# Narrower expert token blocks, weight rests by an adding DMA, and a shifted decode schedule in an attention, MoE and SoLU kernel

## The chip, the core and the metric

The kernel runs as one program on one core of a Trainium2 chip. Its time is the device time of that core in microseconds (us); lower is better. Engines are named as in the profile: PE is the matrix engine (PEld its weight loads), DVE the vector engine, ACT the scalar engine, POOL the GpSimd engine, SP the engine that here only issues DMAs.

## What is computed

Three stages in a row on 1536 tokens of width 384: a linear attention with decay, a mixture of eight experts of which each token goes to one, and a SoLU block. In short:

```python
# attention: per head a 48x48 state, y_t = r_t @ (state + u*k_t v_t), state = w*state + k_t v_t
logits = x @ w_gate                      # 1536 x 8
e = argmax(logits); gate = softmax(logits)[e]
disp[e, 0:count_e] = x[tokens of e]      # at most capacity = 384 tokens for one expert
h = relu(disp @ w1)                      # per expert 384 -> 1024
y = h @ w2                               # per expert 1024 -> 384
x2 = gate * y, back in the tokens' order
h2 = x2 @ w_in; s = h2 * softmax(h2)     # w_in, w_out are stored as float64
out = (layernorm(s) * g_ln) @ w_out
```

With the inputs used, the eight experts get 193, 174, 187, 195, 184, 203, 209 and 191 tokens.

## The kernel before

**Number form.** Float32 values are split into a rounded part `hi` (type F32R, a float32 type that PE takes in one pass) and a rest `lo`, also F32R. A product is three matmuls: hi times hi, hi times lo, lo times hi. So weights, tokens and the hidden layer all need a `hi` (made by ACT) and a `lo` (raw minus hi, made by DVE or POOL).

**Experts.** Every expert works on W = 256 columns, that is, slots for 256 tokens; tokens above W would be done by `overflow()`, which runs only if an expert has more than W. The work is cut into 32 groups g (eight experts, four groups of 256 hidden units each). The loop has steps g = 0 to 33. In step g stand:

- `mm1(g)`: 18 matmuls of 256 columns into `hps`; ACT makes `hh` from it (relu), DVE `hl`.
- `mm2(g - 2)`: 18 matmuls of 256 columns from `hh`, `hl` into `yps`. At the last group of an expert ACT and DVE write `yThi` and `yTlo`, at a column that is read from a register.
- `split_q(1, g + 4)` and `split_q(2, g + 2)`: ACT makes `whi` (L109), DVE or POOL `wlo` (L111) of one 128x768 piece of w1 and of w2. Of the w2 pieces every other one has its `wlo` from POOL, 16 in the program with one of w1; the other 48 are DVE's.
- `xe_split(e + 1)` once an expert (at step 2 for expert 1, then at every second step of an expert): PE transposes the next expert's gathered tokens (`xt`), ACT and DVE make `xhi` and `xlo`. `load_xe` gathers the tokens with an indirect DMA from POOL; its row numbers `ids` come from DRAM, where the last attention block's scatter puts them.
- `load_half`: a 768 KB half of an expert's w1 or w2 into one of four `raw` buffers, from SP.
- `load_piece`, `decode_early`, `decode_piece`: the float64 words of w_in and w_out, 16 pieces of 384 KB, are loaded (two buffers), turned by two ACT operations and four DVE operations into float32 (`da`), and split into `w_hi` and `w_lo`. Piece p is loaded at step 2p - 1, behind the weights of that step on SP (the first two from ACT), its ACT operations come at step 2p + 1, its DVE operations at step 2p + 2. The first step that decodes is step 2, the last 32.
- small work: memsets of `yT` and the scatters `inv` from POOL, position sums from DVE.

Order on each engine is the order of the code, written out by hand; every engine takes its instructions in that order, so an instruction that waits holds up all behind it on its engine. PSUM has four buffers shared by `hps` and `xt`, and two for `yps`.

**Before and after the experts.** Attention takes 12 blocks of 128 tokens; in it six weight pieces of the first expert are split already. The SoLU block takes 12 tiles: `h2` (18 matmuls of 512 columns), softmax and norm, eight transposes `st`, and `out2` (24 matmuls of 384 columns).

Of the kernel before, what the change touches and what calls it, by code (L numbers as in the profile page):

```python
# [24 lines left out]
KF = DF // 128  # L25
W = 256
WARM = 14
# [6 lines left out]
def rwkv_moe_solu_kernel(  # L34
# [20 lines left out]
    NX = NE * RS  # L55
    YW = N + W

# [18 lines left out]
    tot = const.tile([128, NE], F32, name="tot")  # L76
    NB = RS // 128
    ids = const.tile([128, NE, NB], I32, name="ids")

    def load_ids(a, b, c=0, d=2):  # L80
        s = idx.rearrange("(e b p) o -> p e (b o)", p=128, b=NB)
        for i in range(c, d):
            nc.sync.dma_start(out=ids[:, a:b, i], in_=s[:, a:b, i])

    def load_xe(e, r0, nb, rows=N + 1):
        t = xe_p.tile([128, nb, DM], F32, tag="xe", name=f"xe{e}_{r0}", bufs=1)
        for b in range(nb):
            c = r0 // 128 + b
            nc.gpsimd.indirect_dma_start(  # L89
                out=t[:, b, :], out_offset=None, in_=xs[0:rows, :],  # L90
                in_offset=bass.IndirectOffsetOnAxis(ap=ids[:, e, c:c + 1], axis=0), bounds_check=rows - 1, oob_is_err=False,
            )
        return t
# [10 lines left out]

    def split_q(kind, g, pool_lo, defer=False):
        raw = raw_t[kind, g // 2][:, (g % 2) * 768:(g % 2 + 1) * 768]
        hi = wsp.tile([128, 768], F32R, tag=f"hi{kind}", name=f"whi{kind}_{g}")
        lo = wsp.tile([128, 768], F32R, tag=f"lo{kind}", name=f"wlo{kind}_{g}")
        S.activation(hi, raw, AF.Copy)  # L109
        def low():  # L110
            (G if pool_lo else V).tensor_tensor(lo, raw, hi.bitcast(F32), ALU.subtract)  # L111

        if not defer:
            low()
        n = 3 if kind == 1 else 2
        (w1s if kind == 1 else w2s)[g] = tuple(t.rearrange("p (a f) -> p a f", a=n) for t in (hi, lo))
        return low


    def attention(actx):  # L120
# [470 lines left out]
        m = NM - 1  # L591
        x0 = ps_s.tile([128, KD, W], F32, tag="s", name="x0")

# [13 lines left out]
        for kk in range(KD):  # L607
            for bb in range(2):
                T.matmul(
                    x0[:, kk, bb * 128:(bb + 1) * 128], xe0[:, bb, kk * 128:(kk + 1) * 128], ident,  # L610
                    is_transpose=True, start=kk % 2 == 0 and bb == 0, stop=False, skip_group_check=True,
                )
# [30 lines left out]
    def experts_and_solu():  # L643
# [85 lines left out]
        def xe_split(e, t):  # L729
            hi = xe_p.tile([128, KD, W], F32R, tag="xhi", name=f"xhi{e}")  # L730
            lo = xe_p.tile([128, KD, W], F32R, tag="xlo", name=f"xlo{e}")
            for bb in range(2):
                ps = ps_t.tile([128, KD, 128], F32, tag="t", name=f"xt{e}_{bb}")
                for kk in range(KD):
                    T.transpose(ps[:, kk], t[:, bb, kk * 128:(kk + 1) * 128], ident)
                sl = slice(bb * 128, (bb + 1) * 128)
# [64 lines left out]
        def load_piece(p, eng=nc.sync):  # L801
            t = dec_p.tile([128, 384, 2], I32, tag="w64", name=f"w64_{p}")
            s = (w_in if p < NP else w_out).rearrange("p a f -> p (a f)").bitcast(I32)
            j = p % NP
            eng.dma_start(out=t.rearrange("p n c -> p (n c)"), in_=s[:, j * 768:(j + 1) * 768])
            pieces[p] = t
# [10 lines left out]
        def decode_piece(p):  # L817
            raw = pieces.pop(p)
            low, high = raw[:, :, 0], raw[:, :, 1]
            a = dec_p.tile([128, 384], I32, tag="da", name=f"da{p}")  # L820
# [35 lines left out]
        xraw = load_xe(1, 0, 2)  # L856
        dec = None
        for g in range(NQ + 2):
            e, q = divmod(g, 4)
            if q == 0 and e + 1 < YW // W:  # L860
                for n in range(2):
                    for x in range(2):
                        G.memset(yT[x][n][:, :, (e + 1) * W:(e + 2) * W].bitcast(F32), 0.0)
            if g < NQ:
# [3 lines left out]
                if g < 2:  # L868
                    split_q(2, g + 2, not g)
            if g >= 2:  # L870
                mm2(g - 2)
                if g + 2 < NQ:
                    split_q(2, g + 2, g % 2 == 0)
            if q == (1 if e else 2) and e + 1 < NE:
                xe_split(e + 1, xraw)
                if e + 2 < NE:
                    xraw = load_xe(e + 2, 0, 2)
            if g % 2 and g < NQ:
                j = (g + 1) // 2
# [11 lines left out]
            if g == 9 + NM:  # L891
                G.dma_start(out=inv_sb, in_=inv.rearrange("(m p) o -> p (m o)", p=128))
            if g in (1, 2):
                load_piece(g - 1, S)
            if g == 2:
                load_half(1, 4, S)
            if dec:
                decode()
            if g == 2 or g % 2 and 3 <= g <= 4 * NP:
                decode_early((g - 1) // 2)  # L900
            if g % 2 == 0 and 2 <= g < 2 + 4 * NP:
                dec = decode_piece(g // 2 - 1)
                decode()
            if g % 2 and 3 <= g and g // 2 + 1 < 2 * NP:
                load_piece(g // 2 + 1)

# [123 lines left out]
        def overflow():  # L1030
            load_ids(0, NE, 2, NB)
            for e in range(NE):
# [99 lines left out]
```

## Time and profile before

| | |
|---|---|
| median of 3 runs | 374.98 us (372.25 to 375.23) |
| the profiled execution's own time | 369.29 us |
| its span, first to last instruction | 367.5 us, mean granted clock 0.985 |
| PE, PEld busy | 338.4, 303.9 us |
| DVE, ACT, POOL busy | 261.8, 188.6, 173.1 us |
| bytes moved | 53.49 MB, mean 146 GB/s |

Busy time is the time in which an engine has at least one instruction under way. Matmuls overlap, so a busy PE is best judged by the distance between the starts of its matmuls. `ns` is the mean duration of one instruction, `xN` how many of them a row stands for. In a timeline a row begins with its start in us from the span's start and its length in us; in square brackets stands how long the engine was idle ahead of it, and what it waited for. Most reading is done in the stretch from 91 to 245.5 us, where the experts run.

### The profile page before, as it was taken

To read this page: it belongs to the slowest core of one execution; us is meant where nothing else is said; L and a number is where in the kernel's file an instruction comes from. 1 tells how busy PE (TensorE), PEld (TensorE's weight loads), DVE (VectorE), ACT (ScalarE), POOL (GpSimd) and SP (SyncE) were. 2 spreads that over 40 slices of the span, in tenths; PEclk is the share of its full clock that TensorE was granted. 3 is DMA by queue.
4 is the path that set the end of the run, shared out by engine and by line. 5 is a ranking of instruction groups with operands and counts; after the bars stand their busy time and mean duration, and the time that the engine had idled before them with its cause. 6 is when DMAs were issued, how large, how long until landed. Compare 5 with 4: busy or idle time off the path is not lost.

```text
span 367.5 us, 7165 instructions
## 1 busy us (share of the span) xinstructions
PE 338.4 (92%) x2637; PEld 303.9 (83%) x2637; DVE 261.8 (71%) x567; ACT 188.6 (51%) x400; POOL 173.1 (47%) x202
## 2 busy tenths in 40 slices
PE   6889999998969999999998979999999999999970
PEld 2567776766869999999998979998899999999970
DVE  8888898975648999899889989965755444444400
ACT  1355546664636777557566486532465444444410
POOL 7957778854392725567767222201343333333420
PEclk9999999999989999999999999999999999999995
DMA  6957999834367655896988755100000000000010
GB/s 227 353 176 229 254 366 310 211 108 164 49 249 265 229 210 135 185 284 173 259 218 232 244 201 172 47 0 1 2 16 29 21 21 23 22 23 21 22 51 22
DMA packets 17996, 53.49 MB, mean 146 GB/s; under 512 B 5729, under 2 KB 7394, under 8 KB 17954
## 3 DMA queue, kind: packets, MB, share of 16 engines
q1 hardware_dynamic: 14914, 45.86, 41.4%
q0 software_dynamic: 2608, 5.53, 4.6%
q10 hardware_dynamic: 432, 1.57, 1.2%
q8 instruction: 23, 0.38, 0.5%
q14 instruction: 19, 0.16, 0.2%
HBM read 48.21 MB, written 4.74 MB: 144 GB/s over the span
## 4 chain that ended last, share of the span: by engine, by line
PE 46%; DVE 27%; DMA 10%; issue 8%; POOL 2%; ACT 2%; SPq 1%; POOLq 0%; DVEq 0%; ACTq 0%
PE h L929 14%; PE hps L756 7%; DVE wlo L111 6%; PE o L997 3%; PE o L998 3%; PE o L999 3%; DMA w<-in_w_in 3%; PE yps L743 3%; PE yps L744 3%; PE yps L742 3%; PE st L988 2%; DVE w_lo L841 2%; DVE hl L763 2%; DMA u_sb<-in_u 2%; DVE A L286 2%
## 5 line engine op out<-in xcount | busy, mean ns | idle before, releaser
L111 POOL TENSOR_TENSOR wlo<-raw,whi 128x768 fp32r<-128x768 f32 x16 | 30.1, 1885 | 53.3 <-ACT whi L109 51.0
L743 PE MATMUL yps<-hl,whi 128*128 128x256 f32 x192 | 54.5, 284 | 0.1
L742 PE MATMUL yps<-hh,whi 128*128 128x256 f32 x192 | 54.4, 283 | 0.0
L744 PE MATMUL yps<-hh,wlo 128*128 128x256 f32 x192 | 54.4, 283 | 0.0
L109 ACT ACTIVATE whi<-raw 128x768 fp32r<-128x768 f32 x64 | 52.1, 840 | 3.8 <-PE yps L743 3.3
L963 POOL TENSOR_SCALAR e<-e,nmu 128x1024 f32<-128x1024 f32 x12 | 13.5, 1125 | 75.7 <-DVE nmu L962 75.7
L111 DVE TENSOR_TENSOR wlo<-raw,whi 128x768 fp32r<-128x768 f32 x48 | 46.5, 981 | 0.9 <-ACT whi L109 0.6
L940 DVE TENSOR_REDUCE nm<-h 128x1 f32<-128x1024 f32 (+1 forms) x13 | 14.8, 1141 | 33.2 <-PE h L929 33.2
L743 PEld LDWEIGHTS yps<-hl,whi 128*128 128x128 f32 x192 | 36.9, 192 | 0.3 <-DVE hl L763 0.3
L744 PEld LDWEIGHTS yps<-hh,wlo 128*128 128x128 f32 x192 | 36.9, 192 | 0.0
L742 PEld LDWEIGHTS yps<-hh,whi 128*128 128x128 f32 x192 | 36.9, 192 | 0.0
L756 PE MATMUL hps<-xhi,whi 128*128 128x256 f32 x192 | 30.2, 294 | 4.4 <-DVE hl L763 4.0
L997 PE MATMUL o<-w_hi,shi 128*128 128x384 f32 x96 | 33.1, 345 | 0.0
L998 PE MATMUL o<-w_lo,shi 128*128 128x384 f32 x96 | 32.2, 335 | 0.0
L999 PE MATMUL o<-w_hi,slo 128*128 128x384 f32 x96 | 32.2, 335 | 0.0
L756 PEld LDWEIGHTS hps<-xhi,whi 128*128 128x128 f32 x192 | 25.9, 196 | 5.7 <-DVE hl L763 5.0
L763 DVE SCALAR_TENSOR_TENSOR hl<-hps,hh 128x512 fp32r<-128x512 f32 x32 | 22.3, 698 | 10.1 <-ACT hh L762 8.4
L89 POOL DMA_INDIRECT xe<-xs,ids x16 | 20.9, 1305 | 17.5 <-DMA ids<-idx 9.3
L756 PE MATMUL hps<-xhi,wlo 128*128 128x256 f32 x192 | 28.3, 284 | 0.0
L756 PE MATMUL hps<-xlo,whi 128*128 128x256 f32 x192 | 28.3, 283 | 0.0
L756 PEld LDWEIGHTS hps<-xhi,wlo 128*128 128x128 f32 x192 | 25.5, 193 | 0.0
L756 PEld LDWEIGHTS hps<-xlo,whi 128*128 128x128 f32 x192 | 25.3, 192 | 0.0
(182 smaller groups left out, 835.4 us busy)
## 6 DMA issues: line engine op xcount, KB each, us to landing
raw<-in_w SPq DMA_DIRECT2D x31, 768.0 KB
kvr<-in_kvr SPq DMA_DIRECT2D x12, 576.0 KB
rkT<-in_rkT SPq DMA_DIRECT2D x12, 512.0 KB
w<-in_w_out SPq DMA_DIRECT2D x8, 384.0 KB
xs<-xg SPq DMA_DIRECT2D x12, 192.0 KB
w<-in_w_in SPq DMA_DIRECT2D x6, 384.0 KB
w<-in_w_in ACTq DMA_DIRECT2D x2, 384.0 KB
raw<-in_w ACTq DMA_DIRECT2D x1, 768.0 KB
```

Source lines behind the costliest of these rows:

```text
L89: nc.gpsimd.indirect_dma_start(out=t[:, b, :], out_offset=None, in_=xs[0:rows, :], in_offset=bass.IndirectOffsetOnAxis(ap=ids[:, e, c:c + ...
L109: S.activation(hi, raw, AF.Copy)
L111: (G if pool_lo else V).tensor_tensor(lo, raw, hi.bitcast(F32), ALU.subtract)
L742: T.matmul(ps, w[0][ws], x[0][xsl], start=first, stop=False, skip_group_check=True)
L743: T.matmul(ps, w[0][ws], x[1][xsl], start=False, stop=False, skip_group_check=True)
L744: T.matmul(ps, w[1][ws], x[0][xsl], start=False, stop=last, skip_group_check=True)
L756: T.matmul(ps[:, f], w1s[g][i][:, kk, wf], x[j][:, kk], start=not (i or j or f or kk), stop=j == 1 and kk == KD - 1, skip_group_check=True,)
L763: V.scalar_tensor_tensor(hl, ps, 0.0, hh.bitcast(F32), ALU.max, ALU.subtract)
L929: T.matmul(ps[j], col(x, kk, ts_), wi[w][:, kk, fs], start=not (i or kk), stop=i == 2 and kk == KD - 1,)
L997: T.matmul(ps, hi[:, f % 4], wo[0][:, f], start=f == 0, stop=False)
L998: T.matmul(ps, hi[:, f % 4], wo[1][:, f], start=False, stop=False)
L999: T.matmul(ps, lo[:, f % 4], wo[0][:, f], start=False, stop=f == KF - 1)
```

## The change

`W` becomes 224 and a token block is cut into 128 and 96 rows (`BW`). All `hps`, `yps`, `hh`, `hl`, `xhi`, `xlo` and `yT` blocks follow: 224 columns where 256 stood. No expert has more than 209 tokens, so `overflow()`, which would now have two blocks instead of one, doesn't run in either kernel.

`split_q` has a new way for the rest, `by_dma`: ACT makes `hi` and then a second piece, `lo` = minus the raw value rounded in the same way, and a DMA from POOL's queue adds the raw weights from DRAM onto `lo`. Eight pieces are made so: one in attention, and w2 pieces 6, 10, ... 30 (issued at g = 4, 8, ... 28). All others are DVE's: 56 against 48, and POOL makes none.

Float64 pieces have three buffers; pieces 0 and 1 are loaded from SP ahead of the loop, piece p at step 2p - 3 ahead of that step's weights; their ACT operations come at step 2p - 1 and DVE's at step 2p, two steps sooner. Expert 1's `xe_split` moves from step 2 to step 3, and in step 4 `mm2(2)` stands ahead of `mm1(4)`.

```diff
-W = 256
+W = 224
+BW = (128, W - 128)
...
-    def split_q(kind, g, pool_lo, defer=False):
+    def split_q(kind, g, by_dma, defer=False):
...
         S.activation(hi, raw, AF.Copy)
         def low():
-            (G if pool_lo else V).tensor_tensor(lo, raw, hi.bitcast(F32), ALU.subtract)
+            if by_dma:
+                s = (w1 if kind == 1 else w2)[g // 4, :, g // 2 % 2, (g % 2) * 768:(g % 2 + 1) * 768]
+                G.dma_start(out=lo, in_=s, accum_op=ALU.add)
+            else:
+                V.tensor_tensor(lo, raw, hi.bitcast(F32), ALU.subtract)
+        if by_dma:
+            S.activation(lo, raw, AF.Copy, scale=-1.0)
...
-            for bb in range(2):
-                ps = ps_t.tile([128, KD, 128], F32, tag="t", name=f"xt{e}_{bb}")
+            for bb, n in enumerate(BW):
+                ps = ps_t.tile([128, KD, n], F32, tag="t", name=f"xt{e}_{bb}")
                 for kk in range(KD):
-                    T.transpose(ps[:, kk], t[:, bb, kk * 128:(kk + 1) * 128], ident)
+                    T.transpose(ps[:, kk], t[0:n, bb, kk * 128:(kk + 1) * 128], ident[0:n, 0:n])
...
-            t = dec_p.tile([128, 384, 2], I32, tag="w64", name=f"w64_{p}")
+            t = dec_p.tile([128, 384, 2], I32, tag="w64", name=f"w64_{p}", bufs=3)
...
+        load_piece(0)
+        load_piece(1)
         for g in range(NQ + 2):
...
+            if g == 4:
+                mm2(g - 2)
             if g < NQ:
                 mm1(g)
                 if g + 4 < NQ:
                     split_q(1, g + 4, False)
                 if g < 2:
-                    split_q(2, g + 2, not g)
+                    split_q(2, g + 2, False)
             if g >= 2:
-                mm2(g - 2)
+                if g != 4:
+                    mm2(g - 2)
                 if g + 2 < NQ:
-                    split_q(2, g + 2, g % 2 == 0)
-            if q == (1 if e else 2) and e + 1 < NE:
+                    split_q(2, g + 2, g % 4 == 0)
+            if q == (1 if e else 3) and e + 1 < NE:
                 xe_split(e + 1, xraw)
...
+            if g % 2 and g // 2 + 2 < 2 * NP:
+                load_piece(g // 2 + 2)
...
-            if g in (1, 2):
-                load_piece(g - 1, S)
...
-            if g == 2 or g % 2 and 3 <= g <= 4 * NP:
-                decode_early((g - 1) // 2)
-            if g % 2 == 0 and 2 <= g < 2 + 4 * NP:
-                dec = decode_piece(g // 2 - 1)
+            if g % 2 == 0 and g < 4 * NP:
+                if not g:
+                    decode_early(0)
+                dec = decode_piece(g // 2)
                 decode()
-            if g % 2 and 3 <= g and g // 2 + 1 < 2 * NP:
-                load_piece(g // 2 + 1)
+            if g % 2 and g // 2 + 1 < 2 * NP:
+                decode_early(g // 2 + 1)
```

What this does to the order of instructions, at three places. First PE, around expert 1's transposes `xt`; `hps` rows are `mm1`, `yps` rows are `mm2`. Before, where step 2 ends and step 3 begins:

```order
L744 MATMUL yps_1_1627<-hh_1550,wlo_0_930 128x256
L735 MATMUL xt_0_1652<-ident,xe_0_1520 128x128 x3
L735 MATMUL xt_1_1658<-ident,xe_0_1520 128x128 x3
L756 MATMUL hps_1687<-xhi_1466,whi_3_1238 128x256 x6
L756 MATMUL hps_1687<-xhi_1466,wlo_3_1239 128x256 x6
L756 MATMUL hps_1687<-xlo_1467,whi_3_1238 128x256 x6
L742 MATMUL yps_2_1626<-hh_1583,whi_1_1035 128x256
```

Of the change, where step 3 ends and step 4 begins (of step 4's 18 `yps` matmuls the first three stand here):

```order
L754 MATMUL yps_1_1649<-hl_1601,whi_1_1035 128x224
L755 MATMUL yps_1_1649<-hh_1600,wlo_1_1036 128x224
L746 MATMUL xt_0_1736<-ident,xe_0_1521 128x128 x3
L746 MATMUL xt_1_1742<-ident,xe_0_1521 128x96 x3
L753 MATMUL yps_2_1648<-hh_1640,whi_2_1563 128x224
L754 MATMUL yps_2_1648<-hl_1641,whi_2_1563 128x224
L755 MATMUL yps_2_1648<-hh_1640,wlo_2_1564 128x224
```

The transposes stand one step (36 matmuls) later, behind group 1's `mm2`, and group 2's `mm2` follows them, not a `mm1`.

Second POOL, from expert 1's token gather on; before:

```order
L89 DMA xe_0_1520<-xs,ids 128x384 x2
L863 MEMSET yThi_1503 128x2x256
L863 MEMSET yTlo_1505 128x2x256
L863 MEMSET yThi_1504 128x256
L863 MEMSET yTlo_1506 128x256
L111 TENSOR_TENSOR wlo_2_1559<-raw_1_927,whi_2_1558 128x768
L111 TENSOR_TENSOR wlo_4_1647<-raw_2_1341,whi_4_1646 128x768
L89 DMA xe_0_1664<-xs,ids 128x384 x2
```

Of the change, from the second gather (expert 2's) on:

```order
L92 DMA xe_0_1748<-xs,ids 128x384
L92 DMA xe_0_1748<-xs,ids 96x384
L876 MEMSET yThi_1504 128x2x224
L876 MEMSET yTlo_1506 128x2x224
L876 MEMSET yThi_1505 128x224
L876 MEMSET yTlo_1507 128x224
L118 DMA wlo_6_1816<-in_w 128x768
L92 DMA xe_0_1902<-xs,ids 128x384
```

Where POOL had a subtraction of 128x768 in every second step it now has a DMA issue of that size in every fourth.

Third SP, from the row numbers `ids` of experts 1 and later on (`w` are float64 pieces, `raw` expert weights); before:

```order
L83 DMA ids<-idx 128x1x1 x2
L83 DMA ids<-idx 128x6x1 x2
L102 DMA raw_3_1595<-in_w 128x1536
L102 DMA raw_5_1736<-in_w 128x1536
L102 DMA raw_4_1738<-in_w 128x1536
L805 DMA w_2_1745<-in_w_in 128x768
```

Of the change:

```order
L85 DMA ids<-idx 128x1x1
L85 DMA ids<-idx 96x1x1
L816 DMA w_0_1528<-in_w_in 128x768
L816 DMA w_1_1530<-in_w_in 128x768
L85 DMA ids<-idx 128x6x1
L85 DMA ids<-idx 96x6x1
L816 DMA w_2_1612<-in_w_in 128x768
L105 DMA raw_3_1614<-in_w 128x1536
L816 DMA w_3_1755<-in_w_in 128x768
```

Two float64 pieces stand ahead of the row numbers of experts 2 to 7, and from then on each piece stands ahead of its step's weights.

## Rows read from the trace of the kernel before

**Rows 1.** Windows: stretch, its length, busy us PE, PEld, DVE, ACT, POOL, clock, DMA.

```profile
91.00:105.00 14.00, 9.89 (x76) 9.50 (x77) 7.01 (x13) 6.64 (x11) 6.95 (x8) 0.95 0.45 129
105.00:178.00 73.00, 73.00 (x604) 72.89 (x602) 67.56 (x116) 49.08 (x87) 41.34 (x41) 0.99 0.72 215
178.00:245.50 67.50, 63.42 (x517) 62.03 (x516) 60.19 (x87) 40.24 (x71) 23.55 (x19) 1.00 0.59 173
245.50:367.50 122.00, 110.54 (x601) 100.51 (x600) 52.76 (x105) 47.69 (x90) 35.44 (x49) 0.97 0.06 21
```

**Rows 2.** Timeline of PE: matmuls of 256 columns.

```profile
152.88 0.28 PE L742 MATMUL yps<-hh,whi 128*128 128x256 f32 x1
...
153.48 0.28 PE L744 MATMUL yps<-hh,wlo 128*128 128x256 f32 x1
```

**Rows 3.** Groups by shape: one of the six kinds of expert matmul.

```profile
L742 PE MATMUL yps<-hh,whi 128*128 128x256 f32 x192 | 54.4, 283 | 0.0
```

**Rows 4.** Timeline of PE: matmuls of 384 and of 512 columns.

```profile
301.92 0.34 PE L997 MATMUL o<-w_hi,shi 128*128 128x384 f32 x1
...
303.48 0.33 PE L997 MATMUL o<-w_hi,shi 128*128 128x384 f32 x1
...
247.08 0.85 PE L929 MATMUL h<-w_hi,yTlo 128*128 128x512 f32 x3
...
249.13 0.61 PE L929 MATMUL h<-w_hi,yTlo 128*128 128x512 f32 x2
```

**Rows 5.** Transposes of 128 columns: timeline of PE, and their group by shape.

```profile
299.98 1.03 PE L988 MATMUL st<-ident,e 128*128 128x128 f32 x8
...
L988 PE MATMUL st<-ident,e 128*128 128x128 f32 x96 | 12.4, 272 | 0.0
```

**Rows 6.** Chain around expert 1's tokens, and a window behind it (columns of rows 1).

```profile
97.74 6.49 DMA xe<-xs,ids
...
104.28 1.54 PE xt L735 x6
105.82 2.73 PE hps L756 x18
...
104.30:105.50 1.20, 1.20 (x7) 1.19 (x7) 0.00 (x0) 0.28 (x1) 1.20 (x1) 0.50 0.00 0
```

**Rows 7.** Timeline of PE: another expert's transposes.

```profile
155.04 0.82 PE L735 MATMUL xt<-ident,xe 128*128 128x128 f32 x6
```

**Rows 8.** Waits of PE's weight loads, 91 to 245.5 us: total, times, longest.

```profile
PEld hps L756 <- DVE hl L763: 5.0, 5, 1.4
PEld xt L735 <- DMA xe<-xs,ids: 4.3, 1, 4.3
```

**Rows 9.** Timelines of POOL and DVE: the same subtraction beside POOL's, and alone.

```profile
154.78 1.89 POOL L111 TENSOR_TENSOR wlo<-raw,whi 128x768 fp32r<-128x768 f32 x1 [4.02 <-ACT whi L109]
...
154.88 2.21 DVE L841 TENSOR_TENSOR w_lo<-da,w_hi 128x384 fp32r<-128x384 f32 x1
...
115.14 0.55 DVE L841 TENSOR_TENSOR w_lo<-da,w_hi 128x384 fp32r<-128x384 f32 x1
```

**Rows 10.** Groups by shape on DVE, 91 to 245 us.

```profile
L841 DVE TENSOR_TENSOR w_lo<-da,w_hi 128x384 fp32r<-128x384 f32 x8 | 11.1, 1391 | 0.0
L837 DVE SCALAR_TENSOR_TENSOR w_lo<-da,g_sb,w_hi 128x384 fp32r<-128x384 f32 x7 | 10.7, 1535 | 0.1
L785 DVE TENSOR_TENSOR yTlo<-yps,yThi 128x512 f32 x6 | 4.1, 685 | 0.0
L785 DVE TENSOR_TENSOR yTlo<-yps,yThi 128x256 f32 x6 | 2.5, 416 | 0.0
```

**Rows 11.** Chain: two `wlo` of DVE in a row, and the slowest float64 load.

```profile
150.18 1.74 DVE wlo L111 x2
...
152.36 10.10 DMA w<-in_w_in
```

**Rows 12.** Timeline of ACT: two `whi` in a row.

```profile
96.51 1.57 ACT L109 ACTIVATE whi<-raw 128x768 fp32r<-128x768 f32 x2
```

More of the change, by code (lines that the diff above doesn't have):

```diff
@@ L55, in rwkv_moe_solu_kernel @@
     NX = NE * RS
-    YW = N + W
+    YW = N + max(W, 128 * NOV)
     const = ctx.enter_context(tc.tile_pool(name="const", bufs=1))
@@ L76, in rwkv_moe_solu_kernel, with load_xe @@
     tot = const.tile([128, NE], F32, name="tot")
-    NB = RS // 128
+    NB = 2 + NOV
     ids = const.tile([128, NE, NB], I32, name="ids")
     def load_ids(a, b, c=0, d=2):
-        s = idx.rearrange("(e b p) o -> p e (b o)", p=128, b=NB)
+        s = idx.rearrange("(e r) o -> r (e o)", r=RS)
         for i in range(c, d):
-            nc.sync.dma_start(out=ids[:, a:b, i], in_=s[:, a:b, i])
-    def load_xe(e, r0, nb, rows=N + 1):
-        t = xe_p.tile([128, nb, DM], F32, tag="xe", name=f"xe{e}_{r0}", bufs=1)
+            r0, n = (i * 128, BW[i]) if i < 2 else (W + (i - 2) * 128, 128)
+            nc.sync.dma_start(out=ids[0:n, a:b, i], in_=s[r0:r0 + n, a:b])
+    def load_xe(e, c0, nb, rows=N + 1):
+        t = xe_p.tile([128, nb, DM], F32, tag="xe", name=f"xe{e}_{c0}", bufs=1)
         for b in range(nb):
-            c = r0 // 128 + b
+            c = c0 + b
+            n = BW[c] if c < 2 else 128
             nc.gpsimd.indirect_dma_start(
-                out=t[:, b, :], out_offset=None, in_=xs[0:rows, :],
-                in_offset=bass.IndirectOffsetOnAxis(ap=ids[:, e, c:c + 1], axis=0), bounds_check=rows - 1, oob_is_err=False,
+                out=t[0:n, b, :], out_offset=None, in_=xs[0:rows, :],
+                in_offset=bass.IndirectOffsetOnAxis(ap=ids[0:n, e, c:c + 1], axis=0), bounds_check=rows - 1, oob_is_err=False,
             )
@@ L591, in attention @@
         m = NM - 1
-        x0 = ps_s.tile([128, KD, W], F32, tag="s", name="x0")
+        x0 = ps_s.tile([128, KD, 256], F32, tag="s", name="x0")[:, :, 0:W]
         wps = ps_y.tile([128, 512], F32, tag="y", name="wps1")
@@ L607, in attention @@
         for kk in range(KD):
-            for bb in range(2):
+            for bb, n in enumerate(BW):
                 T.matmul(
-                    x0[:, kk, bb * 128:(bb + 1) * 128], xe0[:, bb, kk * 128:(kk + 1) * 128], ident,
+                    x0[:, kk, bb * 128:bb * 128 + n], xe0[0:n, bb, kk * 128:(kk + 1) * 128], ident[0:n, 0:n],
                     is_transpose=True, start=kk % 2 == 0 and bb == 0, stop=False, skip_group_check=True,
@@ L731, in xe_split @@
             lo = xe_p.tile([128, KD, W], F32R, tag="xlo", name=f"xlo{e}")
-            for bb in range(2):
-                ps = ps_t.tile([128, KD, 128], F32, tag="t", name=f"xt{e}_{bb}")
+            for bb, n in enumerate(BW):
+                ps = ps_t.tile([128, KD, n], F32, tag="t", name=f"xt{e}_{bb}")
                 for kk in range(KD):
-                    T.transpose(ps[:, kk], t[:, bb, kk * 128:(kk + 1) * 128], ident)
-                sl = slice(bb * 128, (bb + 1) * 128)
+                    T.transpose(ps[:, kk], t[0:n, bb, kk * 128:(kk + 1) * 128], ident[0:n, 0:n])
+                sl = slice(bb * 128, bb * 128 + n)
                 S.activation(hi[:, :, sl], ps, AF.Copy)
@@ L819, in decode_piece @@
             low, high = raw[:, :, 0], raw[:, :, 1]
-            a = dec_p.tile([128, 384], I32, tag="da", name=f"da{p}")
+            a = dec_p.tile([128, 384], I32, tag="da", name=f"da{p}", bufs=1)
             af = a.bitcast(F32)
@@ L857, in experts_and_solu @@
         dec = None
+        load_piece(0)
+        load_piece(1)
         for g in range(NQ + 2):
             e, q = divmod(g, 4)
-            if q == 0 and e + 1 < YW // W:
+            if q == 0 and (e + 1) * W < YW:
                 for n in range(2):
                     for x in range(2):
-                        G.memset(yT[x][n][:, :, (e + 1) * W:(e + 2) * W].bitcast(F32), 0.0)
+                        G.memset(yT[x][n][:, :, (e + 1) * W:min((e + 2) * W, YW)].bitcast(F32), 0.0)
+            if g == 4:
+                mm2(g - 2)
             if g < NQ:
@@ L1040, in overflow @@
                 for o in range(NOV):
-                    xo = load_xe(e, W + 128 * o, 1)
+                    xo = load_xe(e, 2 + o, 1)
                     ps = ps_t.tile([128, KD, 128], F32, tag="t", name=f"oxt{e}_{o}")
@@ L1113 @@
         "wg": wgp.reshape(128, HP, NE),
-        "w1": inputs["moe_w1"].reshape(NE, KD, 128, 4, W).transpose(0, 2, 3, 1, 4).reshape(NE, 128, 2, 1536),
+        "w1": inputs["moe_w1"].reshape(NE, KD, 128, 4, DF // 4).transpose(0, 2, 3, 1, 4).reshape(NE, 128, 2, 1536),
         "w2": inputs["moe_w2"].reshape(NE, KF, 128, DM).transpose(0, 2, 1, 3).reshape(NE, 128, 2, 1536),
```

## The prediction

> **What bounds the kernel now.** I read the stretches first, then the distance between matmuls, then who waits for whom. By stretches the experts take 91 to 245.5 us, 154.5 of the 367.5 us, and SoLU 122 [rows 1]. In the middle of the experts PE has no idle time at all (73.00 of 73.00 us), DVE is busy for 67.56 of the same 73. So PE sets the pace and DVE is close behind.
>
> How much PE work is that? Matmuls of 256 columns start every 0.120 us: five distances in 0.60 us [rows 2]. There are six kinds of 192, 1152 in all [rows 3], so 138.2 us, and 42 transposes at about 0.108 us, 4.5 us. Of 154.5 us that leaves 11.8 us. The waits name two items: PE stood 4.3 us for expert 1's tokens, and five times, 5.0 us together, for DVE's `hl` [rows 8]. The first has an aftermath: behind the wait the granted clock was 0.50, the 1.2 GHz level, where it is 0.99 over the stretch [rows 1, 6], so the six transposes took 1.54 us where another expert's take 0.82, and the 18 matmuls behind them 2.73 us where 18 x 0.120 is 2.16 [rows 6, 7]. The tokens thus cost 4.3 + 0.7 + 0.6 = 5.6 us.
>
> DVE is slower than it need be. A subtraction of 128x384 takes 0.55 us alone and 2.21 us while POOL does its own [rows 9]; the groups have means of 1.39 and 1.54 us for 8 and 7 of them [rows 10].
>
> **The change, part by part.** The sum is made against the profiled execution's own 369.3 us, of which 1.8 us lie outside the span. The median of the runs shown is 375.0 us, 5.7 us more; I take the difference in time off the median.
>
> *224 columns.* What does a matmul of 224 columns cost? 384 columns start every 0.173 us and 512 every 0.228 us (nine distances in 1.56 and in 2.05 us) [rows 4]. Each 128 columns cost 54 ns, 0.42 ns a column, all the way down to 256; the line gives 106.6 ns at 224. But each matmul has its own weight load. Transposes, which have half the columns and the same 128x128 weights, start no closer than (1.03 - 0.27) / 7 = 0.108 us [rows 5]. I take 110 ns, just above that floor: 10 ns x 1152 = 11.5 us. Bounds: nothing, if these weights already hold a matmul to 120 ns; 13.4 x 1152 = 15.4 us, if the line holds. The page "TensorE: Matmul & The Clock Gate" of the Trainium skill, section "Back-to-back issue gap", has pairs of weight load and matmul start every 81 ns or so at 128 columns. The transposes' 108 ns disagree with it; by that rule weights would not bind here, and the sum would be 21.5 us in all instead of 17.6, 353.5 us.
>
> *Expert 1's tokens a step later.* Before, PE arrived at the transposes at about 99.9 us and the tokens at 104.2 [rows 6, 8]. Now 36 matmuls more stand ahead: 36 x 0.110 = 4.0 us later, less 72 x 0.010 = 0.7 us gained so far, so 103.2 us. If the tokens land as before, a wait of 1.0 us is left and the clock has no reason to fall: gain 4.6 us. Bounds 0 (the two float64 loads that SP now issues ahead of experts 2 to 7's row numbers delay the tokens as much) and 5.6. The `mm2` put between the transposes and `mm1(4)` covers the `xhi` and `xlo` of expert 1: 18 x 0.110 = 2.0 us.
>
> *DVE.* It gets eight more `wlo` among the experts, 0.87 us each, as two in a row take 1.74 us [rows 11]: 7.0 us. POOL's subtractions are gone: if 15 `w_lo` return to 0.55 us, that is 8 x 0.84 + 7 x 0.98 = 13.6 us less. Narrower tiles: 256 columns fewer take 269 ns off `yTlo` [rows 10], 1.05 ns a column; 64 fewer on 32 `hl`, 96 fewer on seven `xlo` and eight pairs of `yTlo` make 3.7 us. DVE goes from 134.8 us busy in the three stretches [rows 1] to 134.8 + 7.0 - 13.6 - 3.7 = 124.5. PE's own work goes from 142.7 to 126.7 + 4.5 = 131.2 us. DVE's share of PE's work stays at 0.95, so its lags stay too, though without the 2.2 us lumps. Of the 5.0 us of waits for `hl` I take off 1.5; bounds: all 5.0 gained, or 3 lost.
>
> *ACT* gets seven negated copies, 0.79 us each (two copies of that size in 1.57 us) [rows 12]: 5.5 us on top of 96 in a stretch that then lasts 137. It stays below three quarters busy: nothing.
>
> *The adding DMAs.* Seven among the experts, 0.39 MB each. One issued in step g is read in step g + 4, at least three steps of 36 x 0.110 = 4.0 us later: 12 us of cover. No such DMA is in the trace. The nearest from POOL's queue, the token gather, lands 6.5 us after its issue [rows 6]; the slowest load of the same size, queued behind two weight halves, took 10.1 us [rows 11]. Both are under 12: I take nothing; the bound above is a rival, and below nothing there is none, since nobody waits for `wlo` now. The traffic rises by 2.8 MB and the stretch shortens: 29.2 MB in 154.5 us become 32 in 137, 234 GB/s, where 215 GB/s kept the DMA engines 0.72 busy [rows 1]. It fits.
>
> *Float64 words.* They go ahead of the weights and have a third buffer, so ACT should not stand for a load as it did at the 10.1 us one [rows 11]. PE had no wait there: no term. Attention and SoLU keep their work.
>
> Sum: 11.5 + 4.6 + 1.5 = 17.6 us; 369.3 - 17.6 = 351.7 us for a run like the profiled one, **357.4 us** for the median.
>
> **The rivals.** *Weights bind (0.12).* The matmul stays at 120 ns, and the change does not do what its narrower columns say. For it: nothing in the trace of this float type is narrower than 256, and the transposes are of another kind. Against: 256 lies on the line of 384 and 512 to within 1 ns. Gain 4.6 + 1.5 = 6.1 us, 368.9 us.
>
> *DVE takes over (0.14).* Before, DVE was idle for 154.5 - 134.8 = 19.7 us of the stretch. If that idle time stays, the stretch lasts 124.5 + 19.7 = 144.2 us: gain 10.3, 364.7 us. For it: conversion starts two steps sooner, when DVE also has all of the first `wlo`. Against: much of the idle time was waiting for PE.
>
> *Narrow matmuls are slower (0.06).* If PE took the columns of this type twice below 256, 224 would cost 2 x 224 x 0.42 + 13 = 201 ns: 81 x 1152 = 93 us lost, some 462 us. It decides early: with 6.1 us from the other terms, the kernel is over 1% slower from (6.1 + 3.8) / 1152 = 8.6 ns more, 129 ns. The line through three widths speaks against it, but none of them is below 256.
>
> *The additions come late (0.08).* Every us over 12 costs up to seven. 14.5 us eats the gain; at 16 us the kernel takes 375.0 - 17.6 + 28 = 385 us. For it: the DMA must read its target as well as its source. The Trainium skill speaks for it too: its page "SBUF — State Buffer", section "A bandwidth-pool intuition that's wrong (but worth ruling out)", tells of a DMA from GpSimd's queue that takes several times longer beside a DVE copy, as its descriptors cannot be written. The gather's 6.5 us fell beside DVE's work too and stays within the cover.
>
> **How the numbers follow.** The forecast has 0.60, the rivals 0.14, 0.12, 0.08 and 0.06. The forecast's own best case is 15.4 + 5.6 + 5.0 = 26 us, 349 us; the DVE and weights rivals end at 369. So 349 to 370 us leaves out the last two and some tails. A measurement here can tell about 1% (3.8 us) from no change. Faster: 0.60, 0.13 of the DVE case, 0.09 of the weights case, 0.01 of late additions: 0.83. Within 1%: 0.01 + 0.03 + 0.04 = 0.08. Slower: 0.06 + 0.03 = 0.09.
>
> **What would show it.** Right: matmuls of 224 columns start every 107 to 112 ns; the transposes of expert 1 wait about 1 us and run at full clock; `w_lo` at 0.55 to 0.6 us throughout; no PE wait for an adding DMA; the experts' stretch at about 137 us; SoLU still 122. Wrong: 120 ns or more between matmuls, PE waits for `hl` above 8 us, or PE waits whose releaser is `wlo` from a DMA.

## The result and the profile after

| | before | changed |
|---|---|---|
| median, same chip | 373.62 us | 361.93 us (359.02 to 365.26) |
| profiled execution, own time | 369.29 us | 362.09 us |
| its span, granted clock | 367.5 us, 0.985 | 360.4 us, 0.968 |

The ratio is 0.966, with an interval of 0.957 to 0.976: faster by 11.7 us in the medians, where 17.6 were forecast; the two profiled executions, which the traces show, are 7.1 us of span apart. Some executions, of most kernels here, take about one to two per cent longer at a lower granted clock: ratios here and below compare executions without that, so that they can differ from the quotient of the medians, and the traces of a2, e4 and e7 below are of such executions. The time lies in the range of 349 to 370 us. But the experiments show that the gain comes by another way than the prediction worked out.

Windows of the changed kernel, with the columns of [rows 1]: the stretch ahead of the experts, the experts in three stretches (cut at 109 and 178 us), and SoLU.

```profile
84.00:95.20 11.20, 7.74 (x39) 6.35 (x39) 3.75 (x17) 2.87 (x8) 6.17 (x6) 0.70 0.32 116
95.20:109.00 13.80, 13.76 (x108) 13.76 (x109) 10.12 (x24) 9.35 (x18) 3.38 (x6) 0.87 0.55 141
109.00:178.00 69.00, 66.67 (x585) 66.49 (x585) 62.58 (x123) 51.43 (x93) 30.00 (x38) 0.98 0.91 264
178.00:237.00 59.00, 56.46 (x505) 56.10 (x503) 47.20 (x78) 37.83 (x68) 14.43 (x19) 1.00 0.69 190
237.00:360.40 123.40, 110.61 (x601) 100.58 (x600) 52.05 (x104) 47.19 (x89) 35.52 (x49) 0.96 0.06 21
```

The experts take 141.8 us where they took 154.5, SoLU 123.4 where it took 122, and the experts begin at 95.2 us instead of 91.0. So, of these two executions, 12.7 us were gained, 4.3 lost ahead of the experts and 1.4 in SoLU. The DMA engines went from 0.72 to 0.91 of their time in the middle.

Timeline of PE (start, length), matmuls of 224 columns; it answers [rows 2]:

```profile
149.80 0.27 PE L755 MATMUL yps<-hh,wlo 128*128 128x224 f32 x1
...
151.14 0.27 PE L755 MATMUL yps<-hh,wlo 128*128 128x224 f32 x1
```

Twelve distances in 1.34 us: 0.112 us each, against 0.120 at 256 columns. On 1152 matmuls that is 9.2 us.

Waits of PE's weight loads (total, times, longest), which answer [rows 8]:

```profile
PEld x L620 <- DMA xe<-xs,ids: 3.7, 2, 2.1
PEld yps L755 <- DMA wlo<-in_w: 2.7, 1, 2.7
PEld hps L767 <- DVE xlo L749: 2.5, 1, 2.5
```

Both waits of rows 8 are gone, the tokens' 4.3 us and the five for `hl`. Three others are there: for expert 0's tokens, ahead of the experts, for an adding DMA, and for expert 1's `xlo`. Behind the last one the clock fell, as it had fallen behind the tokens' wait before. On the chain that ended last:

```profile
115.49 4.57 PE hps L767 x24
```

The granted clock was 0.51 from 115.7 to 119.2 us, and the first 18 of these matmuls took 3.7 us, where 18 x 0.112 is 2.0. The sum over the experts: 9.2 (columns) + 5.6 (tokens, with what came behind them) + 5.0 (`hl`) - 2.5 - 2.7 - 1.8 (a clock of 0.87 over 13.8 us) - 1.7 (the half clock behind `xlo`) = 11.1 of the 12.7 us; 1.6 us stay unassigned.

Nobody waits for a float64 word any more. Tile `w` of the changed kernel: its ACT copies, its loads, and who waited for it (total us, times; both waits are for the conversion, not for a load):

```profile
L824 ACT ACTIVATE w<-w x16: 551/562/582, 101.1 to 226.6; 128x384 int32<-128x384 uint32 x16
...
who waited for it (us, times):
  ACT w_hi L846: 1.0, 1
  DVE hl L774: 0.6, 1
```

In the kernel before, ACT stood 13.6 us for it, seven times. The prediction gave that part of the change no term.

### The profile page after: what moved, and what is told of

Same layout as the page of the kernel before. It is cut to its first block, busy times and chain, and to the rows that moved or that the text cites. A ratio compares the mean times of both kernels' runs of the same rounds, so it can differ in the third digit from the quotient of the medians.

```text
span 360.4 us, 7184 instructions
## 1 busy us (share of the span) xinstructions
PE 331.7 (92%) x2636; PEld 298.1 (83%) x2637; DVE 246.0 (68%) x575; ACT 191.3 (53%) x408; POOL 148.6 (41%) x198
## 4 chain that ended last, share of the span: by engine, by line
PE 50%; DVE 14%; issue 14%; DMA 10%; POOL 6%; ACT 1%; POOLq 0%; SPq 0%; DVEq 0%; ACTq 0%
PE h L945 14%; PE hps L767 8%; DMA wlo<-in_w 5%; PE o L1013 3%; PE o L1014 3%; PE o L1015 3%; PE yps L755 3%; DVE wlo L120 3%; PE yps L753 3%; PE yps L754 3%; PE st L1004 2%; POOL inv L732 2%; DVE A L297 2%; PE yp L326 2%; DMA kvr<-in_kvr 1%
## 5 line engine op out<-in xcount | busy, mean ns | idle before, releaser
L755 PE MATMUL yps<-hh,wlo 128*128 128x224 f32 x192 | 53.0, 276 | 2.5 <-DMA wlo<-in_w 2.5
L120 DVE TENSOR_TENSOR wlo<-raw,whi 128x768 fp32r<-128x768 f32 x56 | 52.5, 961 | 4.0 <-ACT whi L114 2.9
L753 PE MATMUL yps<-hh,whi 128*128 128x224 f32 x192 | 52.8, 275 | 0.0
L754 PE MATMUL yps<-hl,whi 128*128 128x224 f32 x192 | 52.5, 273 | 0.0
L118 POOL DMA_DIRECT2D wlo<-in_w x8 | 7.7, 968 | 56.6 <-ACT wlo L123 56.6
L767 PE MATMUL hps<-xlo,whi 128*128 128x224 f32 x192 | 27.6, 281 | 2.3 <-DVE xlo L749 2.3
L767 PE MATMUL hps<-xhi,whi 128*128 128x224 f32 x192 | 28.6, 286 | 0.4 <-ACT xhi L643 0.4
L774 DVE SCALAR_TENSOR_TENSOR hl<-hps,hh 128x448 fp32r<-128x448 f32 x32 | 20.9, 652 | 10.7 <-ACT hh L773 7.0
L767 PE MATMUL hps<-xhi,wlo 128*128 128x224 f32 x192 | 27.9, 283 | 0.0
L773 ACT ACTIVATE hh<-hps 128x448 fp32r<-128x448 f32 x32 | 17.4, 542 | 16.5 <-PE hps L767 14.9
```

The costliest lines, as they stand in the source:

```text
L120: V.tensor_tensor(lo, raw, hi.bitcast(F32), ALU.subtract)
L753: T.matmul(ps, w[0][ws], x[0][xsl], start=first, stop=False, skip_group_check=True)
L754: T.matmul(ps, w[0][ws], x[1][xsl], start=False, stop=False, skip_group_check=True)
L755: T.matmul(ps, w[1][ws], x[0][xsl], start=False, stop=last, skip_group_check=True)
L767: T.matmul(ps[:, f], w1s[g][i][:, kk, wf], x[j][:, kk], start=not (i or j or f or kk), stop=j == 1 and kk == KD - 1, skip_group_check=True,)
L774: V.scalar_tensor_tensor(hl, ps, 0.0, hh.bitcast(F32), ALU.max, ALU.subtract)
```

## Experiments

Twelve kernels were timed in three groups, each beside the kernel before on one chip: e1, e5, e2, e3 (before took 370.9 us there), a2, e8, e4, e10 (372.8) and e11, e7, e12, e6 (374.1). "Lead" is worked out from the traces: from the issue of a float64 load to ACT's copy of it, median of the sixteen. "Experts" is the time of the first expert matmul and of the first `h2` matmul in each trace; the changed kernel's own trace, of the first section, has 95.2 to 237.0, a lead of 15.5 and no wait.

| kernel | median us | ratio to before, 95% | lead us | ACT's wait for float64 words | experts us |
|---|---|---|---|---|---|
| before | see above | | 8.2 | 13.6 | 91.0 to 245.5 |
| e1: columns alone | 370.08 | 0.997 (0.992 to 1.003) | 8.2 | 18.0 | 95.1 to 245.5 |
| e5: all but the words | 371.71 | 0.997 (0.992 to 1.002) | 8.1 | 25.7 | 92.6 to 243.8 |
| e4: all, words behind weights | 372.16 | 1.000 (0.994 to 1.006) | 10.6 | 23.7 | 95.2 to 249.6 |
| e8: words alone | 367.79 | 0.995 (0.991 to 0.998) | 15.5 | 4.7 | 88.9 to 239.5 |
| e11: words and columns | 361.61 | 0.970 (0.964 to 0.976) | 15.4 | 4.3 | 91.0 to 237.7 |
| a2: the changed kernel | 358.87 | 0.964 (0.956 to 0.971) | 14.9 | 0 | 96.4 to 236.7 |
| e2: no adding DMA in attention | 358.31 | 0.966 (0.961 to 0.972) | 14.6 | 3.8 | 89.8 to 233.0 |
| e3: GpSimd for the other seven | 361.26 | 0.975 (0.969 to 0.981) | 15.1 | 3.9 | 91.5 to 237.4 |
| e7: no adding DMA at all | 362.02 | 0.958 (0.948 to 0.968) | 14.9 | 4.2 | 93.4 to 237.7 |
| e12: fourteen of them | 365.61 | 0.973 (0.963 to 0.983) | 15.5 | 4.2 | 91.0 to 237.6 |
| e6: tokens as before | 358.64 | 0.962 (0.955 to 0.969) | 14.6 | 3.9 | 91.9 to 232.8 |
| e10: as e2, words two steps later | 357.52 | 0.962 (0.952 to 0.971) | 15.0 | 0 | 90.8 to 231.8 |

### The columns and the float64 words

**e1, columns alone.** The kernel before with this and the blocks that follow from it:

```diff
-W = 256
+W = 224
+BW = (128, W - 128)
```

> The kernel before with 224 columns alone: the matmul blocks, the row numbers and the token gather are cut to 224; the steps, the POOL subtractions and the float64 loads stay as before. Theory (PE sets the pace): the changed kernel starts a matmul of 224 columns every 112 ns, so 8 ns x 1152 = 9.2 us come off 373.6: 364 us, or up to 367 if the waits for DVE's hl grow from 5.0 to about 8 us because POOL's subtractions still hold DVE. Rival (DVE sets the pace): DVE loses only 3.7 us of work, and its 19.7 us of idle time stay: 370 us. A second rival, that half of the gain of the change is the tokens' step, also gives 368 to 370 us, with PE waiting 4 us for the tokens of expert 1.

Measured 370.08 us: no gain that can be told, although its matmuls start every 112 ns too. The number is that of the rivals, their reasons are not: PE doesn't wait for expert 1's tokens in its trace, and e11 below speaks against DVE. Waits of PE's weight loads, and the float64 loads on the chain that ended last (start, us):

```profile
PEld hps L759 <- DVE hl L766: 9.8, 7, 3.8
PEld yps L746 <- DVE hl L766: 4.8, 4, 2.5
...
123.62 8.19 DMA w<-in_w_in
144.83 7.93 DMA w<-in_w_in
172.37 10.46 DMA w<-in_w_out
192.95 10.29 DMA w<-in_w_out
```

PE waited 14.6 us for `hl`, 9.3 us more than before (5.3 with the one of 0.3 us): as much as the columns freed. In this trace the experts begin 4.2 us later than before, and the tokens' wait is gone, so that they end at the same place. And on the chain stand four float64 loads, where one stood before, the 10.10 us of [rows 11].

**e5, all but the words.** The changed kernel with the loads and the conversion of before:

```diff
-        load_piece(0)
-        load_piece(1)
...
-            if g % 2 and g // 2 + 2 < 2 * NP:
-                load_piece(g // 2 + 2)
...
+            if g in (1, 2):
+                load_piece(g - 1, S)
...
+            if g % 2 and 3 <= g and g // 2 + 1 < 2 * NP:
+                load_piece(g // 2 + 1)
```

> The changed kernel with the float64 words loaded and converted as before: two buffers, loads behind the weights, conversion from step 2 on. Theory (the earlier conversion fills DVE in the first steps, so that expert 1's xlo comes late): the PE wait of 2.6 us for xlo and the half clock behind it, 1.6 us, go away; 358 us; ACT waits for the float64 loads again, 10 us or more, which PE doesn't see. Rival (the earlier load matters because a stopped ACT stops PE): PE waits for hh or the weights appear, 4 us or more: 366 us. A third: nothing of it reaches PE, 362 us.

Measured 371.71 us: the rival with the stopped ACT, and stronger than it said; PE's wait is for `hl`, 10.1 us, not for `hh` or the weights. Columns, tokens, adding DMAs and a GpSimd without subtractions together give nothing without the words.

**e4, the order on one queue.** Only the place of one call changes; buffers and conversion stay:

```diff
-            if g % 2 and g // 2 + 2 < 2 * NP:
-                load_piece(g // 2 + 2)
             if g % 2 and g < NQ:
                 j = (g + 1) // 2
...
                     load_half(2, j + 2)
+            if g % 2 and g // 2 + 2 < 2 * NP:
+                load_piece(g // 2 + 2)
```

> The changed kernel with the float64 loads behind the weight loads of the same step on SP's queue, as before; third buffer and early conversion stay. Theory (the place in the queue matters): ACT stands for float64 loads again, 5 us or more, PE waits 3 to 5 us for hl: 364 to 366 us. Rival (the third buffer and the time ahead matter): ACT waits for neither, its 7.9 us for weight loads fall, the adding DMA of 192 us is issued sooner and PE's 2.7 us wait for it goes: 358 to 361 us.

Measured 372.16 us: the theory, but 13.3 us over a2 where it had 3 to 5. The chain of e4, then SP's issues and ACT's work at the same place, then waits of SP's queue and of PE:

```profile
144.85 11.05 DMA w<-in_w_in
...
163.95 0.88 DVE wlo L120
164.84 0.33 SPq L105
165.17 0.05 issue
165.22 11.78 DMA w<-in_w_out
177.00 0.02 issue
177.03 0.02 ACT w L824
...
177.90 0.04 ACT hh L773
...
186.29 12.25 DMA w<-in_w_out
...
163.15 2.03 SPq L105 DMA_DIRECT2D raw<-in_w  x2
165.22 0.43 SPq L816 DMA_DIRECT2D w<-in_w_out  x1
...
177.03 0.54 ACT L824 ACTIVATE w<-w 128x384 int32<-128x384 uint32 x1 [5.50 <-DMA w<-in_w_out]
177.47 0.53 ACT L825 ACTIVATE mag<-w 128x384 bf16<-128x384 f32 x1
177.90 0.52 ACT L773 ACTIVATE hh<-hps 128x448 fp32r<-128x448 f32 x1
...
SPq L105 <- DVE wlo L120: 110.4, 22, 10.4
...
PEld hps L767 <- DVE hl L774: 8.6, 4, 4.1
```

Read from 163.95 on this is a loop through SP, ACT and DVE, on which PE hangs. SP issues in order. A weight load waits for DVE to be done with its buffer's last `wlo` (110.4 us in 22 waits). The float64 load stands behind it, is issued at 165.22 and lands 11.78 us later, with two weight halves ahead of it. ACT works in order too and stands 5.50 us at its copy; behind that copy stands `hh` at 177.90, then comes DVE's `hl`, and PE waits for `hl`. DVE's next `wlo`, which SP waits for, is late with it. So the chain reads as a loop with its own period: its loads start 20.4 and 21.1 us apart, with one more piece between two of them, which makes two pairs of steps, 144 x 0.112 = 16.1 us of PE's work. The experts last 150.4, 151.2 and 154.3 us in e1, e5 and e4, although PE's matmuls there start as close as in the changed kernel, which takes 141.8. In e5 and e4 the clock adds to the waits: it is 0.95 and 0.93 over the experts, where e1 has 0.99 and the changed kernel 0.98. On the chains of these three kernels the float64 loads take 7.1 to 12.9 us; the lead, 8.1 to 10.6 us, doesn't cover that.

In the changed kernel the load of the next word, the second of `w_out`, goes out ahead of that step's weights. SP's issue and ACT's copy:

```profile
158.02 0.47 SPq L816 DMA_DIRECT2D w<-in_w_out  x1
...
175.81 0.58 ACT L824 ACTIVATE w<-w 128x384 int32<-128x384 uint32 x1
```

17.8 us lie between the two, and ACT doesn't wait. SP waits for `wlo` there too, 89.6 us in 21 waits, but the float64 load is out before the wait of its step.

**e8, words alone**, at 256 columns. To make room for the third buffer two small tables lie in `iota_w`, and `mag` and `da` have one buffer (`da` has one in the changed kernel too).

```diff
+            if g % 2 and g // 2 + 2 < 2 * NP:
+                load_piece(g // 2 + 2)
...
-            t = dec_p.tile([128, 384, 2], I32, tag="w64", name=f"w64_{p}")
+            t = dec_p.tile([128, 384, 2], I32, tag="w64", name=f"w64_{p}", bufs=3)
```

> The kernel before, with 256 columns and the subtractions on GpSimd, that takes over only the treatment of the float64 words: loads ahead of the weights, a third buffer, conversion two steps sooner (to find room for the third buffer two small tables lie in a tile that the attention has done with). Theory (ACT stands for a late float64 load, and hh and hl come late behind it): ACT's 13.6 us of waits for these loads go, PE's five waits for hl, 5.0 us, fall under 1.5 us, and the time falls by 3 to 5 us, to 366 to 368 us. Rival (the hl waits came from DVE's slow subtractions beside GpSimd): the waits stay at 4 to 5 us and so does the time, 370 to 371 us.

Measured 367.79 us, a ratio of 0.995: some 2 us, where the theory had 3 to 5. The waits for `hl` fell from 5.0 to 1.6 us. In that the theory is right: 3.4 us of them came from the late words and not from DVE's collisions, which e8 still has (`w_lo` up to 2.3 us). The trace is of an execution of 363.05 us, the shortest of twelve, so its stretches are shorter than the median's. Windows of e8 (columns of rows 1):

```profile
101.00:178.00 77.00, 75.42 (x611) 74.65 (x612) 76.10 (x130) 55.05 (x96) 47.51 (x44) 0.96 0.75 230
178.00:239.40 61.40, 61.40 (x514) 61.21 (x512) 55.84 (x78) 37.21 (x64) 21.15 (x17) 1.00 0.55 158
```

Here PE is full at 256 columns: 61.40 of 61.40 us, and DVE 76.10 of 77.

**e11, words and columns together**, with the GpSimd subtractions and the tokens of before (the edits of e1 and e8 in one kernel, without e8's makeshift for room).

> The kernel before with two parts of the change together: 224 columns and the treatment of the float64 words. Its fifteen subtractions on GpSimd and expert 1's tokens stay as before. Alone, the columns gave 0.3% and the words 0.5%. Theory (the two need each other: the words free PE, the columns give it less to do, and the adding DMAs then take the next limit, DVE, away): with 15 GpSimd subtractions DVE is busy for about 135 us of the experts, so that they last 145 to 148 us: 363 to 366 us, ratio 0.975 to 0.985. Rival (the two simply add): 0.8%, 369 us. Third (the adding DMAs do nothing): as the changed kernel, 0.965.

Measured 361.61 us, 0.970: better than the first theory's 363 to 366 us, and the interval holds the third's 0.965 too. What it rules out is the rival: the two parts gave 0.3% and 0.5% alone and give 3.0% together. DVE has as much work in e11 as in e1 (busy for 136.3 and 134.3 us of the experts), and e1 gained nothing; but PE waits 6.0 us for `hl` instead of 14.6. So it was the loop and not DVE's work that held e1.

### The adding DMAs

**a2** is the changed kernel once more, to stand beside the others.

> The changed kernel itself once more, so that the kernels of this group stand beside it on one chip. If the ratio to the kernel before is steady it takes 0.966 of it, 359 to 362 us; the kernel without the attention's adding DMA, 358.3 us beside another set of runs of before, is then faster by 0 to 3 us.

358.87 us, 0.964: the ratio is steady.

**e2, the attention's weight rest on DVE.**

```diff
-                pend.append(split_q(1 + (i // 2) % 2, 2 * (i // 4) + i % 2, m == NM - 3, defer=True))
+                pend.append(split_q(1 + (i // 2) % 2, 2 * (i // 4) + i % 2, False, defer=True))
```

> The changed kernel with one adding DMA less: the weight rest made in the attention is subtracted on VectorE. Theory (the adding DMA stands ahead of expert 0's row numbers): the row numbers land 2.7 us after their scatter instead of 4.5, the tokens of expert 0 are there 3 to 4 us sooner, PE's wait of 3.7 us for them falls under 1.5 us, and the first matmul of the experts starts at 91 to 92 us instead of 95.2: 358 us. Rival (the scatter of the row numbers came late by itself, before the adding DMA was issued): the first matmul still starts at 94 to 95 us, and the time stays at 362 us.

In e2 the first expert matmul starts at 89.8 us instead of 95.2, as the theory says, but the ratios of e2 and a2 are equal. Over all the kernels the start says less. With that adding DMA (the changed kernel, a2, e3 to e6) it lies at 91.5 to 96.4 us, without it at 88.9 to 95.1; the means are 93.8 and 91.4, and the groups overlap. What cost the 4.3 us in the changed kernel stays open.

**e3, GpSimd subtractions for the seven among the experts.**

```diff
-                    split_q(2, g + 2, g % 4 == 0)
+                    split_q(2, g + 2, 2 * (g % 4 == 0))
...
+            if by_dma == 2:
+                G.tensor_tensor(lo, raw, hi.bitcast(F32), ALU.subtract)
```

> The changed kernel with the seven adding DMAs among the experts replaced by subtractions on GpSimd, as the kernel before had them (it had more). Theory (they pay by sparing DVE the shared port): w_lo subtractions beside a GpSimd subtraction take 2.2 us again instead of 0.55, DVE gains about 7 x 1.5 = 10 us of work, and PE waits 3 to 5 us more for hl and xlo: 365 to 367 us. Rival (DVE has slack, and the late adding DMA costs as much): the 2.7 us wait for an adding DMA goes, nothing comes back: 359 to 362 us.

361.26 us: the rival's range, but not its reason, since PE waits 7.5 us for `hl`, which it doesn't in the changed kernel. Beside e2 on the same chip e3 is 2.9 us slower, with intervals that just overlap. Tile `w_lo`, DVE's subtractions (ns, least, median, most) in e3:

```profile
L854 DVE TENSOR_TENSOR w_lo<-da,w_hi x8: 549/553/2205, 108.7 to 170.9; 128x384 fp32r<-128x384 f32 x8
```

In the changed kernel the most is 554 ns. The collisions of [rows 9] come back, fewer than the theory took.

**e7, none at all** (both `by_dma` arguments `False`).

> The changed kernel with no adding DMA and no GpSimd subtraction: all weight rests on VectorE. Theory (DVE is next to the bound): 7 x 0.87 = 6.1 us more for DVE, of which half reaches PE as waits for hl: 361 to 364 us. Rival (DVE has slack once its GpSimd collisions are gone): 357 to 360 us, as with the seven.

**e12, fourteen among the experts instead of seven**, on e2.

```diff
-                    split_q(2, g + 2, g % 4 == 0)
+                    split_q(2, g + 2, g % 2 == 0)
```

> The changed kernel without the attention's adding DMA, but with every second of the second weight's rests among the experts by an adding DMA, fifteen instead of eight. Theory (the DMA engines are at 0.88 to 0.91 between 105 and 178 us with 260 GB/s; 3.1 MB more bring them to their limit): weight loads and additions land late, PE waits 4 us or more for them: 362 to 368 us. Rival (what spares DVE pays): DVE 6 to 7 us less busy, 354 to 357 us.

e7 can't be told from the changed kernel: 0.958 beside 0.964, with intervals that overlap. So the DMAs are not needed for the gain. Getting the work off GpSimd pays something, at the edge of what can be told: with GpSimd subtractions among the experts PE waits 6.0 (e11) and 7.5 us (e3) for `hl`, in the changed kernel, a2, e2, e6, e7, e10 and e12 at most 3.9; the ratios are 0.970 and 0.975 against 0.958 to 0.966 in all of these but e12, and most of the intervals overlap. SoLU takes 122.5 to 123.7 us in the eight traces with adding DMAs among the experts and 121.8 to 122.0 in the six without; why, no run shows.

e12 has 365.61 us, inside what its theory gave, and 0.973, though its interval still overlaps that of e2. (None is in its attention, so there are fourteen in all, against eight in the changed kernel; the expectation counts fifteen.) Its trace has what the theory named, in the middle window and in a wait of PE:

```profile
109.00:178.00 69.00, 67.69 (x609) 67.50 (x608) 62.13 (x120) 55.29 (x99) 36.02 (x43) 1.00 1.02 294
...
PEld yps L755 <- DMA wlo<-in_w: 5.4, 2, 3.2
```

The DMA engines are full (1.02 of their time), and two additions land late.

### The tokens and the start of the conversion

**e6, expert 1's tokens at step 2 as before.**

```diff
-            if g == 4:
-                mm2(g - 2)
...
-            if q == (1 if e else 3) and e + 1 < NE:
+            if q == (1 if e else 2) and e + 1 < NE:
```

> The changed kernel with expert 1's tokens at step 2 and mm2 after mm1, as before. Theory (they come too soon there): PE waits 3 to 4.5 us at the transposes and then runs at half clock, as before: plus 4 to 5 us, 363 us. Rival (the wait only takes the place of the one for xlo): the 3.2 us wait for xlo goes since DVE has a step more, the sum stays within 1.5 us: 358 to 361 us.

358.64 us, 0.962: the rival. The two waits change places. Of e6, in which PE doesn't wait for `xlo`:

```profile
PEld xt L746 <- DMA xe<-xs,ids: 3.6, 1, 3.6
```

The step later gains nothing that can be told.

**e10, conversion from step 2 on**, on e2. The loads come two steps later with it, still in front of the weights and with three buffers.

```diff
-            if g % 2 and g // 2 + 2 < 2 * NP:
-                load_piece(g // 2 + 2)
+            if g % 2 and 3 <= g and g // 2 + 1 < 2 * NP:
+                load_piece(g // 2 + 1)
...
-            if g % 2 == 0 and g < 4 * NP:
-                if not g:
-                    decode_early(0)
-                dec = decode_piece(g // 2)
+            if g == 2 or g % 2 and 3 <= g <= 4 * NP:
+                decode_early((g - 1) // 2)
+            if g % 2 == 0 and 2 <= g < 2 + 4 * NP:
+                dec = decode_piece(g // 2 - 1)
...
-            if g % 2 and g // 2 + 1 < 2 * NP:
-                decode_early(g // 2 + 1)
```

> The changed kernel without the attention's adding DMA, with conversion from step 2 on as before, but with three buffers and the float64 loads two steps ahead and in front of the weights. Theory (what pays is that the word is there when ACT comes to it, and the start at step 0 only costs: ACT stood 3.8 us for the first word, PE 2.7 us for hl and 3.4 us for xlo): these three go and nothing comes back, 352 to 355 us. Rival (conversion two steps sooner is what pays): waits for hl of 5 us or more from the middle of the experts on, 361 to 366 us.

357.52 us: below the changed kernel by less than the intervals tell, and above the theory's 352 to 355. The wait for `xlo` is gone, as the theory says, but 4.4 us at expert 1's transposes took its place. It also shows that the two steps by which conversion starts sooner carry nothing: the lead is 15.0 us here too, and that is what counts. No kernel tried is faster than the changed one by more than the measurement can tell. Whether two buffers would do with the loads in front wasn't tried.

## Why the prediction was right and wrong

The time came out in the range by luck: the two terms that weigh most, the columns and the tokens, bring nothing by themselves that can be told, and the one that the gain hangs on was put at nothing.

**Columns: the size nearly right, the effect not.** 110 ns were taken, 112 measured, 9.2 us for 11.5. The line's 106.6 ns are not reached; why, no run shows. The Trainium skill's 81 ns at 128 columns ("TensorE: Matmul & The Clock Gate", section "Back-to-back issue gap") is not approached: the transposes, of 128 columns, start every 108 ns. But the step "So PE sets the pace and DVE is close behind" failed: 9.2 us less for PE gave 0.3% (e1), because the loop over the late words held the experts at 150 us.

**Float64 words: the step that failed.** "PE had no wait there: no term." PE did wait there, for 3.4 of its 5.0 us by e8, under the name of `hl`. The load of 10.10 us stood on the chain that ended last [rows 11]; the prediction used it as the price of a load, and did not ask who stood behind it. Undoing this part alone takes the whole gain (e5), and so does putting the loads behind the weights (e4); its term is all of it, at these columns.

**`hl`: right in sign, wrong in cause.** "Of the 5.0 us of waits for `hl` I take off 1.5": all 5.0 went. The prediction put them down to DVE's slow subtractions. In e8 these are there and only 1.6 us of the waits are. At 224 columns they do cost waits, 6.0 us in e11 and 7.5 in e3.

**Expert 1's tokens: right in the trace, worth nothing.** The wait of 4.3 us went, and 2.5 us for `xlo` came, with 1.7 us of half clock behind it: "The `mm2` put between ... covers the `xhi` and `xlo`" did not hold, since in the first steps DVE has conversion and all `wlo` at once; with conversion two steps later (e10) there is no such wait. By e6 nothing is left of the term of 4.6 us.

**Adding DMAs.** Their landing was within the 12 us: two of the changed kernel's stand on its chain with 8.8 and 10.1 us, and e2, whose trace has the landing of all seven, gives

```profile
DMA to landing us min/median/max: 4.9/7.5/8.8
```

One was late all the same, by 2.7 us: one of the prediction's own signs of being wrong. The chain shows when it was issued and ACT's timeline why:

```profile
172.48 8.81 DMA wlo<-in_w
...
190.17 0.85 ACT L114 ACTIVATE whi<-raw 128x768 fp32r<-128x768 f32 x1 [4.88 <-DMA raw<-in_w]
190.92 0.83 ACT L123 ACTIVATE wlo<-raw 128x768 fp32r<-128x768 f32 x1
...
192.06 10.11 DMA wlo<-in_w
```

The cover was counted from the step in which the DMA stands in the code. It starts only behind ACT's negated copy, and ACT had stood 4.88 us for a weight load.

**Attention: failed.** "Attention and SoLU keep their work." The first expert matmul came 4.3 us later. The chain ahead of it, first before, then in the changed kernel:

```profile
73.70 3.33 DMA idx<-row,slot
77.04 2.67 DMA ids<-idx
...
73.89 4.82 DMA idx<-row,slot
78.73 4.53 DMA ids<-idx
85.52 4.01 DMA xe<-xs,ids
```

The scatter and the row numbers of expert 0 took some 3.4 us longer, and PE then ran at a clock of 0.70 from 84 to 95.2 us, where it had 1.00 ahead of the experts before.

So the time came out in the range only because the words are part of the change: with its term of nothing for them the prediction would have given e5 and e4 the same 357 us, and missed both by some 14 us. Of the signs it named, the distance of 112 ns, the transposes at full clock and `w_lo` at 0.55 to 0.6 us came; the experts took 141.8 us and not 137.

**The rivals.** "DVE takes over", 364.7 us, was nearer than the forecast: a gain of 10.3 us where 11.7 were measured and 17.6 forecast. Its reason is real in e8, where DVE is busy for 76.10 of 77 us, but not in the changed kernel, with 62.58 of 69. No rival was the late word, though ACT's waits for it lay open in the trace.

## What to carry to other kernels

A wait has a near end and a far end: before a wait for DVE is put down to DVE, follow the releaser back to the load or queue that started it, and see what stands behind that load on an engine that works in order. The lead of a load is counted from when its queue gets to it, not from the step in which it is written: a load that needs no buffer of the busy kind belongs in front of those that wait for one. Where a cycle through the queues is about as long as the busiest engine's work, making that engine faster alone can show nothing, and shortening the cycle alone little: 0.3% and 0.5% here, and 3.0% for both together.

## What the runs showed of the chip

A packet of 3072 bytes took 253 ns of its DMA engine in the adding DMAs and 121 ns in the plain float64 loads (medians in the changed kernel's trace): an addition of 384 KB occupies the DMA engines for twice its bytes. With seven of them among the experts the engines were busy for 0.91 of the middle window at 264 GB/s, with fourteen for 1.02 at 294. A pair of steps takes 72 x 0.112 = 8.1 us and loads two weight halves and one float64 piece, 1.97 MB, so 244 GB/s by loads alone; how near that is to the limit without adding DMAs was not tested. Over the whole stretch of the experts e7, which has none, kept the engines 0.65 busy at 200 GB/s.
